# Attention, experts and a gated layer on one core: the experts' second product token-major with 512 columns moving, batches cut into 256 and 320 tokens, the last sums transposed by blocks

## The chip, the core and the metric

The kernel runs on one core of a Trainium2 chip. The metric is the device time of one execution in microseconds, as the median of several runs. The core has TensorE (PE in the rows; PEld is its weight load), VectorE (DVE), ScalarE (ACT), GpSimd (POOL) and SyncE (SP), each with its own instruction queue in program order; they wait for one another through semaphores. Matmul results go to PSUM, which has eight banks of 512 fp32 columns on 128 partitions.

## What is computed

Four batches of 576 tokens, eight heads of 64. Attention goes through 32 packed queries per head; then four experts with a hidden width of 1024, weighted by token; then a layer of width 2048 with s * relu^2 + b.

```python
def _attn_ref(q, k, v, p):
    p_packed = sm_attn(p, k, v)
    return sm_attn(q, p_packed, p_packed)

def _moe_ref(x, domain_probs, w1, w2):
    p = domain_probs / (domain_probs.sum(-1, keepdims=True) + 1e-09)
    out = np.zeros((N, D), dtype=np.float32)
    for e in range(E):
        h = np.maximum(x @ w1[e], 0.0)
        out += p[:, e:e + 1] * (h @ w2[e])
    return out

def _moe2_ref(x, w_in, w_out, s, b):
    r = np.maximum(x @ w_in, 0.0)
    return (s * (r * r) + b) @ w_out
```

N = 2304 tokens, D = 512, E = 4, F = 1024, d_ff = 2048; inputs fp32.

## The kernel before

Every large product is made of three fp32r matmuls: each operand is split into an upper part (a copy rounded to fp32r) and a lower part (the rest), and high x low, high x high and low x high are added up in PSUM.

The order of all work is written out by hand. The main loop runs over `ua`: expert e, batch bi, half hf of the batch's 576 tokens (288 each), hidden block f of 128, 256 steps in all. In step i it first issues what the table `weave` has for i (`run(i)`), then by `advance()` the first product `m1` of step i + 2, then the second product `m2` of step i. `m1` (line 708): six matmuls with a block of the folded first weight stationary and 288 token columns moving into a bank of two (`h`); ScalarE writes the relu's upper part (line 718), VectorE the lower (line 719). `m2` (line 736): for each of four 128-wide output blocks m three matmuls, a block of the second weight stationary, 288 token columns moving, into four banks `acc0` to `acc3`, which add up over the eight f of a half. The result lies with output features on partitions and tokens in columns.

At a half's last f the four banks are emptied: for expert 0 VectorE multiplies by the token's weight into `x2` (line 760), for later experts into `y` (line 751), and POOL adds `y` to `x2` (line 762). The weights per token lie along the columns, so they are broadcast over all partitions: `expert_weights` (woven into step 3) norms them with four small VectorE operations and writes them to DRAM; `load_pb` loads them, once for every expert and batch, broadcast.

Expert 0's steps are woven with the attention of the next batch: `at_s1` (scores of the packed queries, line 189), `at_exp1`, `at_a1t` (TensorE transposes, line 237), `at_pv`, `at_pt`, `at_s2` (line 306), then on VectorE and POOL `at_s2t` to `at_fin`, which writes the batch's `a2`, the moving operand of `m1`. The halves of `at_s2` to `at_fin` are those of `m1`. Experts 1 to 3 are woven with the folding of the next first weight (lines 502 and 548), the split of the second weight (lines 573, 576) and the preparation of the last layer's weights.

The last layer is `m3` (line 860: seven combinations of quarters of x, 384 columns moving) and `m4` (line 896: 128 tokens stationary, 512 columns of the output weight moving). `m3` starts ten units early (`EARLY`), inside the last ten steps of the main loop; `m4` of a pair of token tiles starts 18 units after its first `m3`. `x_sum` and `xs_parts` (line 804, 805) make `m3`'s operands from `x2`, six tiles of 384 tokens with features on partitions. `gate` queues four operations (ScalarE 814, VectorE 817, ScalarE 824, VectorE 828) in a list `later`, of which `go_on`, called in each `m3`, issues one per entry.

Of the kernel before, what the change touches and what calls it, by code (L numbers as in the profile page):

```python
# [8 lines left out]
F32 = mybir.dt.float32  # L9
# [10 lines left out]
def attention_experts_mlp_kernel(  # L20
# [78 lines left out]
    pn_dram = dram.tile([E, NT], F32, name="pn_dram")  # L99
# [216 lines left out]
    def at_s2t(bi, h, gs=(0, 1)):  # L316
        for g in gs:
            nc.vector.transpose(
                out=stt["sc", bi, h][:, blocks((g,))[0], :32],
                in_=stt.pop(("s2", bi, h, g))[:, :HT],  # L320
# [5 lines left out]

    def at_max2(bi, h, gs=(0, 1), eng=nc.gpsimd):
        j, n = blocks(gs)
        sc = stt["sc", bi, h][:, j, :32]
        m = att.tile([P, NJ, 1], F32, tag="mx", bufs=2, name=f"mx_{bi}{h}{gs[0]}")[:, j, :]  # L330
# [3 lines left out]
    def at_exp2(bi, h, gs=(0, 1)):  # L334
        sc = stt["sc", bi, h][:, blocks(gs)[0], :32]
        nc.scalar.activation(sc, sc, AF.Exp, scale=scale)

    def at_norm2(bi, h, gs=(0, 1), eng=nc.gpsimd):
        j, n = blocks(gs)
        sc = stt["sc", bi, h][:, j, :]  # L340
        r = att.tile([P, NJ, 1], F32, tag="r2", bufs=2, name=f"r2_{bi}{h}{gs[0]}")[:, j, :]
# [8 lines left out]
    def at_a2t(bi, h, gs=(0, 1)):  # L350
        j, n = blocks(gs)
        tag, bufs, size = ("a1", 2, S) if (bi, h) == (0, 0) else ("t", 3, NJ * 33)
# [335 lines left out]
    pb_t = {}  # L688

    def load_pb(e, bi):  # L690
        t = wa.tile([P, S], F32, tag="pb", bufs=2, name=f"pb_{e}{bi}")
        nc.sync.dma_start(
            out=t, in_=pn_dram[e, bi * S : (bi + 1) * S].partition_broadcast(P)
        )
        pb_t[e, bi] = t

    hh = {}

    def hid(dt, tag, bufs, name):
        return wa.tile([P, HT], dt, tag=tag, bufs=bufs, name=name)  # L700

    def m1(e, bi, hf, f):
        t = ps_h.tile([P, 512], F32, tag="h", name=f"h_{e}{bi}{hf}{f}")
        tok = slice(hf * HT, (hf + 1) * HT)
# [11 lines left out]
        xh = hid(F32R, "hh", 3, f"hh_{e}{bi}{hf}{f}")[:, :HT]  # L716
        xl = hid(F32R, "hl", 3, f"hl_{e}{bi}{hf}{f}")[:, :HT]
        nc.scalar.activation(xh, t[:, :HT], AF.Relu)  # L718
        nc.vector.scalar_tensor_tensor(  # L719
            out=xl, in0=t[:, :HT], scalar=0.0, in1=f32(xh), op0=ALU.max, op1=ALU.subtract  # L720
        )
        hh[e, bi, hf, f] = (xh, xl)

    acc = {}
    x2 = {}

    def m2(e, bi, hf, f):
        xh, xl = hh.pop((e, bi, hf, f))
        wh, wl = w2_t[e, f]
        if f == 0:  # L730
            for m in range(KB):
                acc[m] = ps_acc.tile([P, 512], F32, tag=f"acc{m}", name=f"acc_{e}{bi}{hf}{m}")
        for m in range(KB):
            col = slice(m * P, (m + 1) * P)
            for n, (w, x) in enumerate(((wl, xh), (wh, xh), (wh, xl))):
                nc.tensor.matmul(  # L736
                    acc[m][:, :HT],
                    lhsT=w[:, col],
                    rhs=x,
                    start=(f == 0 and n == 0),  # L740
# [561 lines left out]
```

## Time and profile before

| | us |
|---|---|
| median of 3 runs | 1096.07 (1095.29 to 1096.73) |
| the profiled execution | 1094.97 |
| its span, first to last instruction | 1093.2 |
| TensorE busy | 1080.1 |
| VectorE, ScalarE, POOL busy | 670.3, 399.5, 288.7 |

Expert 0's steps run from about 26 to 221 us, the others to 391, 553 and 720, the last layer after that. In a row of a group the mean is the length of one instruction; for overlapping matmuls the distance from start to start in the timeline is what one costs. What stands in brackets at the end of a timeline row is idle time of that engine just before it, and what ended it.

### The profile page before, as it was taken

The page shows a single profiled execution, that of the slowest core. Times are in us where ns is not written, and L with a number is a line of the kernel's source. Part 1 is how long each engine was busy: PE and PEld are TensorE (multiplying, and loading weights), DVE is VectorE, ACT ScalarE, POOL GpSimd, SP SyncE. Part 2 cuts the span into 40 slices and gives each one's busy share as a digit, 9 for nine tenths or more (in the row PEclk, how much of TensorE's full clock was granted, in tenths as well). Part 3 has the DMA queues.
Part 4 walks back from the last instruction along what each step waited for, and adds up shares of the span by engine and source line. Part 5 has one row for each costly group of instructions (what it writes and reads, how often), then busy time and mean ns, then how long its engine had stood idle before and what let it go on. Part 6 is the DMA issues. An engine that isn't in the chain of part 4 may idle for free.

```text
span 1093.2 us, 19304 instructions
## 1 busy us (share of the span) xinstructions
PE 1080.1 (99%) x7588; PEld 1004.6 (92%) x7588; DVE 670.3 (61%) x1235; ACT 399.5 (37%) x798; POOL 288.7 (26%) x344
## 2 busy tenths in 40 slices
PE   8999999999999999999999999999999999999998
PEld 5788889999999999999999999989899999999987
DVE  7875764567566446556456634489845766775555
ACT  3433223553443343433433313255632332342121
POOL 1530203134322244224244343264111120210000
PEclk9999999999999999999999999999999999999999
DMA  9742221133226684774685431346766555655532
GB/s 279 213 131 58 52 85 36 29 100 115 70 66 243 219 228 134 218 231 155 223 220 156 139 98 72 150 165 249 289 200 220 184 205 173 214 205 189 191 116 87
DMA packets 68971, 175.14 MB, mean 160 GB/s; under 512 B 11408, under 2 KB 28048, under 8 KB 68880
## 3 DMA queue, kind: packets, MB, share of 16 engines
q1 hardware_dynamic: 68032, 172.79, 49.3%
q8 instruction: 60, 0.98, 0.4%
q10 hardware_dynamic: 848, 1.11, 0.4%
q14 instruction: 31, 0.25, 0.1%
HBM read 127.44 MB, written 46.44 MB: 159 GB/s over the span
## 4 chain that ended last, share of the span: by engine, by line
PE 94%; DVE 3%; POOL 1%; ACT 1%; issue 1%; DVEq 0%; POOLq 0%; ACTq 0%
PE acc L736 36%; PE h L708 19%; PE o L896 18%; PE h L860 15%; PE pp L502 1%; PE s L189 1%; PE pp L548 1%; PE s L306 1%; PE pv L255 1%; PE pw L400 1%; ACT a L226 1%; PE warm L947 1%; PE tr L237 0%; POOL x L762 0%; DVE kT L150 0%
## 5 line engine op out<-in xcount | busy, mean ns | idle before, releaser
L736 PE MATMUL acc<-hl,w2h 128*128 128x288 f32 x1024 | 303.0, 296 | 0.0
L736 PE MATMUL acc<-hh,w2l 128*128 128x288 f32 x1024 | 302.5, 295 | 0.5 <-POOL w2l L576 0.5
L736 PE MATMUL acc<-hh,w2h 128*128 128x288 f32 x1024 | 302.6, 296 | 0.0
L708 PE MATMUL h<-a,w1p 128*128 128x288 f32 x1536 | 250.4, 298 | 1.1 <-DVE hl L719 0.9
L719 DVE SCALAR_TENSOR_TENSOR hl<-h,hh 128x288 fp32r<-128x288 f32 x256 | 116.3, 454 | 188.8 <-ACT hh L718 187.6
L708 PEld LDWEIGHTS h<-a,w1p 128*128 128x128 f32 x1536 | 216.6, 188 | 16.7 <-issue 11.4
L896 PE MATMUL o<-wo,gg 128*128 128x512 f32 x864 | 223.1, 392 | 1.9 <-DVE gg L828 1.9
L860 PE MATMUL h<-xs,wop 128*128 128x384 f32 x1008 | 203.3, 337 | 0.7 <-DVE y L751 0.7
L736 PEld LDWEIGHTS acc<-hh,w2l 128*128 128x128 f32 x1024 | 192.3, 188 | 0.9 <-POOL w2l L576 0.7
L736 PEld LDWEIGHTS acc<-hl,w2h 128*128 128x128 f32 x1024 | 192.9, 188 | 0.0
L860 PEld LDWEIGHTS h<-xs,wop 128*128 128x128 f32 x1008 | 180.1, 188 | 13.8 <-DVE y L751 1.4
L736 PEld LDWEIGHTS acc<-hh,w2h 128*128 128x128 f32 x1024 | 192.7, 188 | 0.0
L896 PEld LDWEIGHTS o<-wo,gg 128*128 128x128 f32 x864 | 160.2, 188 | 26.3 <-DVE gg L828 2.7
L718 ACT ACTIVATE hh<-h 128x288 fp32r<-128x288 f32 x256 | 104.5, 408 | 213.1 <-PE h L708 206.4
L762 POOL TENSOR_TENSOR x<-x,y 128x288 f32<-128x288 f32 (+2 forms) x144 | 88.6, 651 | 162.4 <-DVE y L751 162.1
L814 ACT ACTIVATE yy<-yy 128x768 f32<-128x768 f32 x48 | 40.2, 838 | 114.6 <-DVE yy L880 114.6
L880 DVE TENSOR_TENSOR yy<-h,uv 128x384 f32<-128x384 f32 x96 | 51.0, 552 | 47.9 <-PE h L860 47.8
L824 ACT ACTIVATE gg<-yy,b_sb 128x768 fp32r<-128x768 f32 x48 | 44.8, 934 | 37.5 <-DVE yy L817 36.2
L828 DVE SCALAR_TENSOR_TENSOR gg<-yy,b_sb,gg 128x768 fp32r<-128x768 f32 x48 | 55.2, 1150 | 1.2 <-ACT gg L824 1.2
L576 POOL TENSOR_TENSOR w2l<-w2r,w2h 128x512 fp32r<-128x512 f32 x32 | 41.8, 1306 | 52.4 <-ACT w2h L573 45.2
L817 DVE SCALAR_TENSOR_TENSOR yy<-yy,s_sb 128x768 f32<-128x768 f32 x48 | 51.2, 1067 | 0.0
L685 POOL TENSOR_TENSOR wo<-wo 128x512 fp32r<-128x512 f32 x16 | 24.0, 1507 | 102.2 <-ACT wo L684 102.2
(374 smaller groups left out, 978.0 us busy)
## 6 DMA issues: line engine op xcount, KB each, us to landing
xs<-xs_dram SPq DMA_DIRECT2D x63, 768.0 KB, 4.3
w1p_dram<-w1o SPq DMA_DIRECT2D x32, 512.0 KB, 3.7
w1p<-w1p_dram SPq DMA_DIRECT2D x128, 128.0 KB, 4.4
xs_dram<-xs SPq DMA_DIRECT2D x21, 768.0 KB, 3.4
w2r<-in_moe_w_dram SPq DMA_DIRECT2D x32, 256.0 KB, 4.8
w1r<-in_moe_w_dram SPq DMA_DIRECT2D x12, 512.0 KB, 5.1
q<-in_q_dram SPq DMA_DIRECT2D x16, 288.0 KB, 7.7
pb<-pn_dram SPq DMA_DIRECT2D x16, 288.0 KB, 4.5
```

Of the source, the lines that this page charges most:

```text
L576: nc.gpsimd.tensor_tensor(out=lo, in0=raw_t.pop((e, f)), in1=f32(hi), op=ALU.subtract)
L708: nc.tensor.matmul(t[:, :HT], lhsT=w1p_block(e, bi, f, gi, w), rhs=a2[bi][:, x, gi, tok], start=(n == 0), stop=(n == 3 * G - 1),)
L718: nc.scalar.activation(xh, t[:, :HT], AF.Relu)
L719: nc.vector.scalar_tensor_tensor(out=xl, in0=t[:, :HT], scalar=0.0, in1=f32(xh), op0=ALU.max, op1=ALU.subtract)
L736: nc.tensor.matmul(acc[m][:, :HT], lhsT=w[:, col], rhs=x, start=(f == 0 and n == 0), stop=(f == NF - 1 and n == 2),)
L762: nc.gpsimd.tensor_tensor(out=dst, in0=dst, in1=y[:, a - t0 : z - t0], op=ALU.add)
L817: nc.vector.scalar_tensor_tensor(out=y, in0=y, scalar=s_sb, in1=y, op0=ALU.mult, op1=ALU.mult)
L824: nc.scalar.activation(t[:, 0], y, AF.Identity, bias=b_sb)
L828: nc.vector.scalar_tensor_tensor(out=t[:, 1], in0=y, scalar=b_sb, in1=f32(t[:, 0]), op0=ALU.add, op1=ALU.subtract)
L860: nc.tensor.matmul(ps, lhsT=w[:, a, col], rhs=x[:, z, m, :], start=(n == 0), stop=(n == 3 * HK - 1),)
L880: nc.vector.tensor_tensor(out=dst, in0=ps, in1=src, op=ALU.add)
L896: nc.tensor.matmul(o_acc[i], lhsT=lhsT, rhs=w, start=(f == 0 and n == 0), stop=(f == FG - 1 and n == 2),)
```

## The change

- `m2` becomes token-major: 128 tokens of the hidden values are stationary, all 512 columns of the second weight's row block move. A bank holds one tile of 128 tokens by 512 features; the four banks are used in rotation.
- 576 is no multiple of 128, so a batch is cut at 256 (even batches: 256 and 320 tokens) or 320 (odd: 320 and 256), and the 64 tokens left at the end of an even batch share a tile with the first 64 of the next. `m1` of these steps writes its hidden values in two pieces; `rest` holds the shared tile's eight blocks. `m2` has six matmuls in a step, and nine in the first half of an odd batch.
- A token's weight now is a value per partition: `p_tok` is made by four TensorE transposes and one ScalarE copy at the end of `expert_weights`, whose VectorE operations work on 18 partitions. The trip through DRAM, `load_pb` and `y` are gone. `m2_out` empties a bank by one VectorE operation, which also adds the sum so far (`xt`).
- In the last expert the sum is written back to PSUM, transposed there by VectorE in 32x32 blocks into `xt`, and `x_turn` moves the blocks by ScalarE copies to their places in `x2`: 16 copies for each of six groups of three tiles, two in each step, queued in `later` and issued at the end of a step.
- `raw0` and `p_rows` take the place of smaller tiles; `x2_0` lies where the first batch's `a2` was.

The diff, cut to what the steps of the prediction speak of (the attention functions take their slices from `part`, `width` and `pieces` in the same way throughout):

```diff
+    def part(bi, h):
+        a = 256 + 64 * (bi % 2)
+        return slice(a * h, a + (S - a) * h)
...
     def at_s2(bi, h, tags="mm"):
...
                     nc.tensor.matmul(
-                        ps[g][half(c ^ bi % 2), :HT],
+                        ps[g][half(c ^ bi % 2), :n],
                         lhsT=stt["sbd", bi, c][half(g), e, :],
-                        rhs=kqT["q", bi, c][half(g), e, h * HT : (h + 1) * HT],
+                        rhs=kqT["q", bi, c][half(g), e, part(bi, h)],
...
     def m1(e, bi, hf, f):
...
-                    t[:, :HT],
+                    t[:, : width(bi, hf)],
                     lhsT=w1p_block(e, bi, f, gi, w),
-                    rhs=a2[bi][:, x, gi, tok],
+                    rhs=a2[bi][:, x, gi, part(bi, hf)],
...
+        todo = [(x, t[:, : 2 * P])]
+        if bi % 2 and not hf:
+            todo = [(x, t[:, 64 : 64 + 2 * P])]
+            todo.append(([y[:, 64:] for y in rest[f]], t[:, :64]))
+        elif hf and not bi % 2:
+            y = wa.tile([P, 2, P], F32R, tag="rest", bufs=NF, name=f"rest_{e}{bi}{f}")
+            rest[f] = y[:, 0], y[:, 1]
+            todo.append(([y[:, :64] for y in rest[f]], t[:, 2 * P : 2 * P + 64]))
+        for (hi, lo), src in todo:
+            nc.scalar.activation(hi, src, AF.Relu)
+            nc.vector.scalar_tensor_tensor(
+                out=lo, in0=src, scalar=0.0, in1=f32(hi), op0=ALU.max, op1=ALU.subtract
+            )
+
+    def m2(e, bi, hf, f):
+        wh, wl = w2_t[e, f]
+        own = hh.pop((e, bi, hf, f))
+        t0 = (bi * S + P // 2 * (bi % 2) + hf * 2 * P) // P
+        do = [(t0 + i, [y[:, i * P : (i + 1) * P] for y in own]) for i in range(2)]
+        if bi % 2 and not hf:
+            do.append((t0 - 1, rest.pop(f)))
+        for j, (xh, xl) in do:
+            if f == 0:
+                n = acc["n"] = (acc.get("n", -1) + 1) % KB
+                acc[j] = ps_acc.tile([P, DM], F32, tag=f"acc{n}", name=f"acc_{e}{j}")
+            for n, (x, w) in enumerate(((xh, wl), (xh, wh), (xl, wh))):
+                nc.tensor.matmul(
+                    acc[j], lhsT=x, rhs=w,
+                    start=(f == 0 and n == 0), stop=(f == NF - 1 and n == 2),
+                )
+            if f == NF - 1:
+                m2_out(e, j)
...
+    def m2_out(e, j):
+        t, p1 = acc.pop(j), p_tok[:, e, j : j + 1]
...
+        dst = x if e < E - 1 else t
         nc.vector.scalar_tensor_tensor(
+            out=dst, in0=t, scalar=p1, in1=x, op0=ALU.mult, op1=ALU.add
+        )
+        if e == E - 1:
+            nc.vector.transpose(out=x, in_=t)
+            done.append(j)
+            if all(NS * i + n in done for n in range(NS)):
+                later.append([(x_turn, i, a, h) for a in range(4) for h in range(2)])
+
+    def x_turn(i, a, h):
...
+        r = slice(32 * a, 32 * a + 32)
+        src = xt[i][r].rearrange("j t (m q c) -> j q m t c", m=KB, q=4)
+        dst = x2[i].rearrange("j m (t b c) -> j b m t c", t=NS, b=4)
+        for q in (2 * h, 2 * h + 1):
+            nc.scalar.activation(dst[32 * q : 32 * q + 32, a], src[:, q], AF.Copy)
...
         def expert_weights():
...
+            dp = p_rows[:NB, 0].rearrange("j (a e) -> j a e", e=E)
+            ds = p_rows[:NB, 2, :P]
+            nc.vector.reduce_sum(ds, dp, axis=AX.X)
+            nc.vector.tensor_scalar(ds, ds, 1e-9, None, ALU.add)
+            nc.vector.reciprocal(ds, ds)
+            pn = p_rows[:NB, 1].rearrange("j (e a) -> j e a", e=E)
             nc.vector.tensor_tensor(
+                out=pn.rearrange("j e a -> j a e"), in0=dp,
+                in1=ds.unsqueeze(2).to_broadcast([NB, P, E]), op=ALU.mult,
+            )
+            t = bank("p_tok")[:, : E * NB].rearrange("a (e j) -> a e j", e=E)
+            for e in range(E):
+                nc.tensor.transpose(t[:, e, :], pn[:, e, :], ident[:NB, :NB])
+            nc.scalar.activation(p_tok, t, AF.Copy)
...
-                at(s0 + 8, load_pb, ne, nb)
...
             m2(*u)
+            if later and i < pos(0):
+                go_on()
             if pos(0) <= i:
                 m3(*ub[i - pos(0)])
```

## Rows read from the trace of the kernel before

**Rows 1.** The page: busy time by engine, granted clock by slice, chain by line.
```profile
PE 1080.1 (99%) x7588; PEld 1004.6 (92%) x7588; DVE 670.3 (61%) x1235; ACT 399.5 (37%) x798; POOL 288.7 (26%) x344
...
PEclk9999999999999999999999999999999999999999
...
PE acc L736 36%; PE h L708 19%; PE o L896 18%; PE h L860 15%; PE pp L502 1%; PE s L189 1%; PE pp L548 1%; PE s L306 1%; PE pv L255 1%; PE pw L400 1%; ACT a L226 1%; PE warm L947 1%; PE tr L237 0%; POOL x L762 0%; DVE kT L150 0%
```

**Rows 2.** Groups by line and shape: instruction, count, busy us, mean ns, idle before.
```profile
L736 PE MATMUL acc<-hl,w2h 128*128 128x288 f32 x1024 | 303.0, 296 | 0.0
...
L896 PE MATMUL o<-wo,gg 128*128 128x512 f32 x864 | 223.1, 392 | 1.9 <-DVE gg L828 1.9
L860 PE MATMUL h<-xs,wop 128*128 128x384 f32 x1008 | 203.3, 337 | 0.7 <-DVE y L751 0.7
```

**Rows 3.** Timeline of PE, 500 to 512 us: start, length, instruction, count.
```profile
500.48 0.96 PE L708 MATMUL h<-a,w1p 128*128 128x288 f32 x6
...
502.87 0.96 PE L708 MATMUL h<-a,w1p 128*128 128x288 f32 x6
```

**Rows 4.** Timeline of PE in the last layer, 734 to 740 and 1074 to 1090.
```profile
734.88 1.20 PE L860 MATMUL h<-xs,wop 128*128 128x384 f32 x6
...
738.42 1.31 PE L896 MATMUL o<-wo,gg 128*128 128x512 f32 x5
...
1073.69 15.80 PE L896 MATMUL o<-wo,gg 128*128 128x512 f32 x69
```

**Rows 5.** Timeline of PE, 222 to 224 us: matmuls of 256 columns.
```profile
223.09 0.28 PE L548 MATMUL pp<-w1h,ptpl 128*128 128x256 f32 x1
...
223.80 0.42 PE L708 MATMUL h<-a,w1p 128*128 128x288 f32 x2
```

**Rows 6.** Timeline of DVE and of PE around step 3, 36 to 46 us.
```profile
36.66 2.28 DVE L150 STREAM_TRANSPOSE kT<-k 128x576 f32<-128x576 f32 x2
...
39.99 0.28 DVE L976 TENSOR_TENSOR pn<-dp,ds 128x72 f32<-128x72 f32 x1
...
38.99 1.19 PE L189 MATMUL s<-kT,pbd 64*64 64x288 f32 x12 [1.50 <-DVE kT L150]
40.11 1.06 PE L708 MATMUL h<-a,w1p 128*128 128x288 f32 x6
```

**Rows 7.** Groups by line and shape: prices of DVE and ACT operations.
```profile
L719 DVE SCALAR_TENSOR_TENSOR hl<-h,hh 128x288 fp32r<-128x288 f32 x256 | 116.3, 454 | 188.8 <-ACT hh L718 187.6
L718 ACT ACTIVATE hh<-h 128x288 fp32r<-128x288 f32 x256 | 104.5, 408 | 213.1 <-PE h L708 206.4 <-DVE sc L318 3.3 <-DVE y L751 2.0
...
L912 DVE TENSOR_TENSOR o_sb<-o,o_sb 128x512 f32<-128x512 f32 x53 | 36.2, 684 | 14.6 <-PE o L896 14.6
...
L573 ACT ACTIVATE w2h<-w2r 128x512 fp32r<-128x512 f32 x32 | 20.1, 632 | 21.1 <-PE acc L736 17.8 <-DMA w2r<-in_moe_w_dram 3.2
...
L355 DVE STREAM_TRANSPOSE at<-sc 128x576 f32<-128x576 f32 x6 | 4.7, 777 | 2.9 <-POOL sc L346 2.9
```

**Rows 8.** Timeline of PE, 34 to 51 us: transposes of the packed attention.
```profile
47.02 0.75 PE L237 MATMUL tr<-ident,a 128*128 128x128 f32 x4 [0.51 <-ACT a L226]
```

**Rows 9.** Timeline, 221 to 230 and 672 to 684 us: two waits of PE.
```profile
228.33 0.37 PE L736 MATMUL acc<-hh,w2l 128*128 128x288 f32 x1 [0.49 <-POOL w2l L576]
...
672.33 4.37 POOL L762 TENSOR_TENSOR x<-x,y 128x96 f32<-128x96 f32 x8 [3.43 <-DVE y L751]
...
680.61 1.06 PE L708 MATMUL h<-a,w1p 128*128 128x288 f32 x6 [0.90 <-DVE hl L719]
```

**Rows 10.** Hand-over: timeline 715 to 743; stretches (PE, PEld, DVE, ACT, POOL busy).
```profile
719.27 1.93 DVE L805 TENSOR_TENSOR xs<-x,xs 128x768 fp32r<-128x768 f32 x1
...
719.72 1.23 PE L860 MATMUL h<-xs,wop 128*128 128x384 f32 x6
...
734.06 0.98 PE L896 MATMUL o<-wo,gg 128*128 128x512 f32 x3 [1.88 <-DVE gg L828]
...
720.00:745.00 25.00, 22.39 (x115) 19.91 (x114) 23.80 (x26) 14.63 (x21) 16.30 (x11) 1.00 0.39 157
```

More of the change, by code (lines that the diff above doesn't have):

```diff
@@ L98, in attention_experts_mlp_kernel, with width @@
     own = att.tile([P, 2, D], F32, name="own")
-    pn_dram = dram.tile([E, NT], F32, name="pn_dram")
+    p_tok = const.tile([P, E, NT // P], F32, name="p_tok")
+    HB = 10
+    XB = NT3
+    def part(bi, h):
+        a = 256 + 64 * (bi % 2)
+        return slice(a * h, a + (S - a) * h)
+    def width(bi, h):
+        t = part(bi, h)
+        return t.stop - t.start
     kq_in, kqT, v_in, pbd = {}, {}, {}, {}
@@ L318, in at_s2t @@
             nc.vector.transpose(
-                out=stt["sc", bi, h][:, blocks((g,))[0], :32],
-                in_=stt.pop(("s2", bi, h, g))[:, :HT],
+                out=stt["sc", bi, h][:, pieces(bi, h, (g,))[0], :32],
+                in_=stt.pop(("s2", bi, h, g))[:, : width(bi, h)],
             )
@@ L325, in blocks, with pieces @@
         return slice(gs[0] * NJ // 2, gs[0] * NJ // 2 + n), n
+    def pieces(bi, h, gs):
+        n = width(bi, h) // 32
+        return slice(gs[0] * n, (gs[0] + len(gs)) * n), len(gs) * n
     def at_max2(bi, h, gs=(0, 1), eng=nc.gpsimd):
[L328 removed]
+        j, n = pieces(bi, h, gs)
         sc = stt["sc", bi, h][:, j, :32]
[L330 removed]
+        m = att.tile([P, 2 * HB, 1], F32, tag="mx", bufs=2, name=f"mx_{bi}{h}{gs[0]}")[:, j, :]
         nc.vector.reduce_max(m.rearrange("a j o -> a (j o)"), sc, axis=AX.X)
@@ L350, in at_a2t @@
     def at_a2t(bi, h, gs=(0, 1)):
-        j, n = blocks(gs)
-        tag, bufs, size = ("a1", 2, S) if (bi, h) == (0, 0) else ("t", 3, NJ * 33)
+        j, n = pieces(bi, h, gs)
+        tag, bufs, size = ("a1", 2, S) if (bi, h) == (0, 0) else ("t", 3, 2 * HB * 33)
         t = att.tile([P, size], F32, tag=tag, bufs=bufs, name=f"at_{bi}{h}{gs[0]}")[:, : n * 32]
@@ L685, in wo_parts @@
         nc.gpsimd.tensor_tensor(out=lo, in0=f32(lo), in1=f32(hi), op=ALU.subtract)
[L688 to L700, printed above, removed]
+    later = []
+    hh, rest, acc, xt, x2 = {}, {}, {}, {}, {}
     def m1(e, bi, hf, f):
         t = ps_h.tile([P, 512], F32, tag="h", name=f"h_{e}{bi}{hf}{f}")
-        tok = slice(hf * HT, (hf + 1) * HT)
         n = 0
@@ L719, in m1 @@
+    done = []
+    def m2_out(e, j):
+        t, p1 = acc.pop(j), p_tok[:, e, j : j + 1]
+        i = j // NS
+        if i not in xt:
+            xt[i] = keep.tile([P, NS, DM], F32, tag="x2", bufs=XB, name=f"xt_{i}")
+        x = xt[i][:, j % NS]
+        if e == 0:
+            nc.vector.tensor_scalar(x, t, p1, None, ALU.mult)
+            return
+        dst = x if e < E - 1 else t
         nc.vector.scalar_tensor_tensor(
-            out=xl, in0=t[:, :HT], scalar=0.0, in1=f32(xh), op0=ALU.max, op1=ALU.subtract
+            out=dst, in0=t, scalar=p1, in1=x, op0=ALU.mult, op1=ALU.add
@@ L721, in m1 @@
         )
[L722 to L740, printed above, removed]
-                    stop=(f == NF - 1 and n == 2),
-                )
-        if f < NF - 1:
-            return
-        t0 = bi * S + hf * HT
-        cuts = sorted({t0, t0 + HT} | {c for c in range(0, NT, T3) if t0 < c < t0 + HT})
-        for m in range(KB):
-            if e > 0:
-                y = hid(F32, "y", 3, f"y_{e}{bi}{hf}{m}")
-                pb = pb_t[e, bi][:, hf * HT : (hf + 1) * HT]
-                nc.vector.tensor_tensor(out=y[:, :HT], in0=acc[m][:, :HT], in1=pb, op=ALU.mult)
-            for a, z in zip(cuts, cuts[1:]):
-                i = a // T3
-                if i not in x2:
-                    x2[i] = keep.tile([P, KB, T3], F32, tag="x2", bufs=NT3, name=f"x2_{i}")
-                dst = x2[i][:, m, a - i * T3 : z - i * T3]
-                src = acc[m][:, a - t0 : z - t0]
-                if e == 0:
-                    pb = pb_t[e, bi][:, a - bi * S : z - bi * S]
-                    nc.vector.tensor_tensor(out=dst, in0=src, in1=pb, op=ALU.mult)
-                else:
-                    nc.gpsimd.tensor_tensor(out=dst, in0=dst, in1=y[:, a - t0 : z - t0], op=ALU.add)
```

56 lines of the change are left out of this document (29 added, 27 removed).

## Prediction

> **What bounds the kernel now.** I read the page from the top: the share of busy time, the granted clock, then the chain that ended last. The reader should see that TensorE is busy for 99% of the span, that its granted clock shows a 9 in all 40 slices (the upper of its two levels, 2.4 GHz), and that the chain lies on TensorE for nearly its whole length: 36% on the second product (line 736), 19% on the first (708) [rows 1]. So the time is the sum of TensorE's periods, and another engine counts only where TensorE waits for it. The row of a group gives 296 ns for a matmul [rows 2], but matmuls overlap, so this is no price. A price is the distance between starts. From one group of six first-product matmuls to the next, a whole step of 6 + 12 matmuls of 288 columns, it is 502.87 - 500.48 = 2.39 us, or 132.8 ns each [rows 3].
>
> **The second product.** Now each of 32 halves (4 experts, 4 batches, 2) has 8 steps of 12: 3072 matmuls of 288 columns, at 132.8 ns 408.0 us. Afterwards there are 4 experts x 8 hidden blocks x 18 token tiles x 3 = 1728 of 512, the same 884,736 columns. The last product (`m4`, line 896) has this very form, 128x128 stationary and 512 moving: 69 in a row take (15.80 - 0.39)/68 = 226.6 ns each, groups of five among other work (1.31 - 0.39)/4 = 230 ns [rows 4]. (0.39 us is the length of one matmul's own row [rows 2].) The new groups are of six or nine, so I take 228.5, between them: 394.8 us. Gain 13.2 us; the ends are 226.6 (16.4) and 230 (10.6).
>
> The Trainium skill, TensorE: Matmul & The Clock Gate, section Back-to-back issue gap, speaks against the change: it gives columns/2.4 + 2.5 ns, 122.5 ns for 288 and 215.8 for 512, so that leaving out 1344 matmuls saves 3.4 us and not 13.2. The trace disagrees at both sizes (132.8 and 226.6 to 230 [rows 3, 4]); what that rule would do to the time is the second rival below.
>
> **The first product.** 1536 matmuls of 288 become 768 of 256 and 768 of 320. Six of 256 columns take 223.80 - 223.09 = 0.71 us, 118 ns each [rows 5]; 384 columns take (1.20 - 0.34)/5 = 172 ns [rows 2, 4]. No row has 320: it lies between 132.8 and 172, on the line from 256 to 384 at 145, and I take 146.5, since that one group of 384 is a short one. 768 x (118 + 146.5) = 203.1 against 204.0: gain 0.9 (a loss of 4 to a gain of 6, if the 320 is off by 6 ns).
>
> **Uneven steps.** A step is now 6 x 118 + 6 x 228.5 = 2.08 us in most halves, 2.25 where 320 columns meet two tiles, and 2.94 where a tile is shared by two batches. What is woven between steps has 0.31 us less cover per short step. Attention of batches 1 and 3 is woven into short steps: TensorE waits at its transposes for ScalarE, 0.51 us [rows 8], and batches 2 and 3 do the same. +0.3 each for 1 and 3; for 2, whose chain lies in long steps, -0.2: +0.4 us.
>
> **The opening.** The expert weights of step 3 now end in four TensorE transposes and a ScalarE copy, ahead of the scores of batch 1 in TensorE's order. VectorE has a queue there: the transposes of k (36.66, 2.28 us) end at 38.94, the weights' own four operations follow and end at 40.27, and the scores that wait for k start at 38.99, the first product at 40.11 [rows 6]. Afterwards those four work on 18 partitions, but on 512, 128, 128 and 512 elements in a row: two at 0.684 [rows 7], two at some 0.33 (between the 0.28 of a small one [rows 6] and 0.684), 2.0 us. Starting at 39.0, behind k's, they end near 41.0; four transposes and the copy, whose bank the scores need, add 0.7 (four of 128 columns take 0.75 [rows 8]); all 16 score matmuls 1.3 (twelve take 1.1 [rows 6]). The first product starts near 43.0, 2.9 later. The savings of steps 0 to 2 (0.93 us) and some 0.1 of a shorter first part vanish in that wait as well: +3.9 us (ends 2 and 6). Behind the waiting transposes stand the scores, the fifth first product and all after them; ScalarE and VectorE get ahead meanwhile, so nothing further is late.
>
> **What goes.** 16 broadcast loads of weights leave SP's queue, and POOL loses its sums at line 762. Today TensorE is held up at 228.33 for 0.49 us, at a half's first product into an accumulator (the row names the split of the second weight, but VectorE is just emptying that bank), and at 680.61 for 0.90, since POOL's eight sums, 4.37 us from 672.33, put off the weight sums that ScalarE waits for ahead of its relu [rows 9]. The new accumulators rotate over four banks with two or three in use, so they are free a half earlier, and the sums are gone: -1.4 us. VectorE's emptying is 18 x 0.684 per expert instead of 32 of 288 columns at some 0.45 [rows 7], nothing on the path. The extra 64-token pieces (one small ScalarE and VectorE operation in half the steps) hide under 2.25 and 2.94 us of TensorE.
>
> **The last expert.** Each tile costs VectorE 0.684 for the sum and 0.70 for the transpose (0.777 for 576 [rows 7]). Then ScalarE turns it, 16 copies of 384 elements on 32 partitions per group of three tiles, two a step; by the operations on 288 (0.408) and 512 (0.632) [rows 7] 0.50 each. They stand in ScalarE's order ahead of the next step's relu (0.408), after which VectorE takes 0.454 [rows 7] before the bank of the first product is free. After three tiles into short steps: VectorE's 3 x 1.38 = 4.15 us begin some 1.1 before the half's end and are done 3.0 after it; two turns, one woven copy, relu and the lower part follow: 3.0 + 1.0 + 0.63 + 0.41 + 0.5 = 5.5, needed at 2 x 2.08 = 4.16: 1.4 us. Two tiles into short steps, without a woven copy: 0.3. Long steps cover it. Together +1.7 (0 to 5).
>
> **The hand-over.** The second product ends at T = 719.72. VectorE is then in a 1.93 us operation until T + 1.5 [rows 10]; two sums and two transposes take it to T + 4.25, and only then can ScalarE begin the last 16 turns, queued ahead of the gates. To the first gate's upper part there are ten turns (5.0) and eight other operations at that stretch's mean, 14.63/21 = 0.70 [rows 10]: T + 14.9; its lower part, at VectorE's mean of 0.92 there: T + 15.8. Today the last product gets it at 734.06, T + 14.3 [rows 10], after waiting 1.88. So +1.5 us there; of the six turns left, 3.0 us, which delay the copies of the next operands, I count 1.8: +3.3 (ends -1 and 6).
>
> **Sum.** -13.2 - 0.9 + 0.4 + 3.9 - 1.4 + 1.7 + 3.3 = -6.2. The profiled execution took 1094.97 (span 1093.2 and 1.8 around it), the runs' median is 1096.07, 1.1 above. So 1088.8 by the profile, 1089.9 as a median. My ends, combined as independent ones, give 1083 to 1098 for this case, chance 0.60.
>
> **Rivals.** (1) The waits of opening, last expert and hand-over are hidden, because queues run ahead elsewhere: -13.2 - 0.9 - 1.4 gives 1080.6. For it: TensorE waits today for only some 13 us of 1093 [rows 1]; against it: the order in the queues is fixed by the program. 0.22. (2) A column costs at 512 what it costs at 288 (132.8/288 = 0.461 ns, 236 ns a matmul): the main gain is nil, 1103. The 226.6 to 230 of [rows 4] speak against it. 0.09. By the 3.4 us of the Trainium skill it would be 1099.7. (3) Slower: ScalarE becomes the bound in the last expert. A short step holds two turns, a relu (0.41) and, in two steps of three, a woven operation of 512 (0.63, so 0.42 on average); it outlasts 2.08 us once a turn costs over 0.62. If copies that cross from one group of 32 partitions to another cost double (1.0), each of 16 short turning steps takes 2.83 instead of 2.08, 12 us, and the hand-over's sixteen another 8: 1110. No row has such a copy across partitions of this size. 0.09.
>
> **How the numbers follow.** The likeliest case gives 1089.9. The range takes in the first rival down to 1079 and the second at 1103; what is left out is the third and part of the first, under 0.2. A measurement of this kernel can tell about 0.2%, or 2.2 us, from no change. Of the forecast's 0.60 0.48 lies under 1093.9, 0.10 within 2.2 us, 0.02 above; rival 1 is faster, 2 and 3 slower: 0.70, 0.10, 0.20.
>
> **What would show it.** The second product's rows: 1728 of 512, 227 to 230 between starts, six in some 1.37 us. First products six in 0.71 or 0.88. A hole in TensorE before the transposes of the expert weights, until about 41, waiting for VectorE. No wait for an accumulator at a half's end. In the last expert, waits of first products for VectorE at starts of short halves. Between 720 and 745 ScalarE near 90% busy, with last products waiting for gates. If the second product's period is over 234, or turning copies cost over 0.6 us, I am wrong.

## The result and the profile after

The changed kernel takes 1111.54 us (median; 1110.32 to 1112.62) beside 1096.4 for the kernel before: 1.0139 times as long, interval 1.0122 to 1.0157. I had forecast 1089.9 and a range up to 1103: wrong in sign, and out of the range. The kernel that the experiments led to takes 1093.15, 0.9978 times the kernel before (0.9968 to 0.9988).

The page of the changed kernel, as [rows 1] and [rows 2] for before:

```profile
span 1108.5 us, 16823 instructions
...
PE 1078.5 (97%) x6248; PEld 918.5 (83%) x6248; DVE 694.3 (63%) x1309; ACT 467.7 (42%) x1023; POOL 198.4 (18%) x200
...
PE 83%; DVE 8%; ACT 5%; issue 2%; DMA 2%; SPq 1%; POOL 0%; ACTq 0%; DVEq 0%
PE acc L755 28%; PE o L929 18%; PE h L717 16%; PE h L893 15%; ACT x L795 1%; PE pp L518 1%; DVE hl L739 1%; PE s L318 1%; DVE xt L778 1%; DMA v<-in_v_dram 1%; ACT hh L738 1%; DVE acc L774 1%; PE pp L564 1%; PE s L200 1%; PE pv L266 1%
...
L755 PE MATMUL acc<-w2h,hh 128*128 128x512 f32 x512 | 201.9, 394 | 0.0
```

The chain by engine in the kernel before:

```profile
PE 94%; DVE 3%; POOL 1%; ACT 1%; issue 1%; DVEq 0%; POOLq 0%; ACTq 0%
```

The chain has left TensorE: 83% of it lies there instead of 94%, 8% is on VectorE and 5% on ScalarE. The second product (now line 755) went from 36% of the chain to 28%; that does not measure its price, which fell by about 10 us of 1100 (below), but shows how much of the chain now runs over other engines. TensorE's own records lost 1.6 us of busy time, and the span grew by 15.3. The new time is waiting, and turns (`ACT x L795`), sums (`acc L774`) and transposes (`xt L778`) stand on the path.

Where it went, by distances between the first second products of the experts. In the kernel before these lie at 30.31, 228.33, 396.31 and 558.20 us. The first row starts at TensorE's first matmul; "hand-over" runs from the end of the second product to the third product's 181st matmul, and the last row from there to the start of the last matmul. The columns to the right are experiments told below (us).

| stretch | before | after | e1 | e3 | e4 | e5 | f1 | f2 | h3 | h4 |
|---|---|---|---|---|---|---|---|---|---|---|
| up to the first | 28.86 | 28.44 | 28.80 | 29.46 | 29.13 | 28.51 | 29.39 | 28.76 | 32.15 | 29.06 |
| expert 0 | 198.02 | 203.62 | 200.52 | 203.22 | 200.29 | 202.84 | 203.14 | 196.67 | 197.86 | 197.08 |
| expert 1 | 167.98 | 168.18 | 168.21 | 168.20 | 168.25 | 168.05 | 168.21 | 168.09 | 168.10 | 168.09 |
| expert 2 | 161.89 | 159.41 | 159.41 | 159.41 | 159.41 | 159.41 | 159.41 | 159.41 | 159.41 | 159.41 |
| expert 3 | 161.51 | 165.19 | 165.04 | 160.67 | 161.68 | 161.41 | 160.86 | 159.72 | 159.52 | 161.70 |
| hand-over | 39.89 | 46.74 | 46.62 | 40.83 | 40.80 | 46.72 | 40.81 | 40.79 | 40.80 | 46.76 |
| last layer | 329.49 | 331.21 | 331.21 | 331.21 | 331.21 | 331.21 | 331.21 | 331.21 | 331.21 | 331.21 |

Expert 2, where TensorE has no wait in either kernel, is 2.5 us shorter: the gain exists. Expert 0 loses 5.6, expert 3 3.7, the hand-over 6.9, the last layer 1.7, and expert 1 gains nothing.

**The steps themselves** came out as worked out. Timeline of TensorE, the last expert (start, length, instruction; the second products between are left out):

```profile
572.98 1.04 PE L717 MATMUL h<-a,w1p 128*128 128x320 f32 x6
575.24 1.04 PE L717 MATMUL h<-a,w1p 128*128 128x320 f32 x6
...
606.88 1.04 PE L717 MATMUL h<-a,w1p 128*128 128x320 f32 x6
609.82 1.04 PE L717 MATMUL h<-a,w1p 128*128 128x320 f32 x6
...
628.82 0.88 PE L717 MATMUL h<-a,w1p 128*128 128x256 f32 x6
630.93 0.88 PE L717 MATMUL h<-a,w1p 128*128 128x256 f32 x6
```

Steps of 2.26, 2.94 and 2.11 us, where I had 2.25, 2.94 and 2.08.

**The opening.** Timeline of VectorE and of TensorE, 36 to 48 us:

```profile
36.29 2.28 DVE L161 STREAM_TRANSPOSE kT<-k 128x576 f32<-128x576 f32 x2
...
38.75 0.65 DVE L1004 TENSOR_REDUCE p_rows<-p_rows 18x128 f32<-18x512 f32 x1
39.43 1.03 DVE L1005 TENSOR_SCALAR p_rows<-p_rows 18x128 f32<-18x128 f32 x1
40.49 0.94 DVE L1006 RECIPROCAL p_rows<-p_rows 18x128 f32<-18x128 f32 x1
41.47 1.02 DVE L1008 TENSOR_TENSOR p_rows<-p_rows 18x512 f32<-18x512 f32 x1
```

```profile
42.63 0.58 PE L1014 MATMUL p_tok<-ident,p_rows 18*128 18x18 f32 x4 [7.00 <-DVE p_rows L1008]
43.15 2.58 PE L200 MATMUL s<-kT,pbd 64*64 64x288 f32 x16
45.66 1.31 PE L717 MATMUL h<-a,w1p 128*128 128x256 f32 x6
```

TensorE idles 7.00 us for the expert weights, and the next 16 score matmuls take 2.58 where twelve took 1.19 [rows 6]: the granted clock fell to 0.5 (1.2 GHz) at 39.59, in that hole, and came back at 46.41. The first product starts at 45.66, 5.55 later than before.

**The last expert.** ScalarE and VectorE, 622 to 628, and the wait that follows on TensorE:

```profile
624.62 1.06 ACT L795 ACTIVATE x<-xt 32x384 f32<-32x384 f32 x2 [4.76 <-DVE xt L778]
625.71 0.38 ACT L738 ACTIVATE hh<-h 128x256 fp32r<-128x256 f32 x1
```

```profile
626.12 0.42 DVE L739 SCALAR_TENSOR_TENSOR hl<-h,hh 128x256 fp32r<-128x256 f32 x1 [1.02 <-ACT hh L738]
```

```profile
626.60 0.98 PE L717 MATMUL h<-a,w1p 128*128 128x256 f32 x6 [0.95 <-DVE hl L739]
```

ScalarE is idle for 4.76 us ahead of two turns, because these wait for VectorE's transpose; the relu behind them (line 738) could have run from 622.16, when the six matmuls that it reads end (start 621.29, 0.87 us), and comes at 625.71. The lower part, the bank, and TensorE follow. One second product waits too, for a bank out of which VectorE transposes, at a half's start:

```profile
600.21 0.47 PE L755 MATMUL acc<-w2l,rest 128*128 128x512 f32 x1 [0.80 <-DVE xt L778]
```

**The hand-over.** The waits of TensorE from 716 to 752 us, then the busy time by stretch (columns as in [rows 10]):

```profile
731.68 9.12 PE L893 MATMUL h<-xs,wop 128*128 128x384 f32 x42 [3.15 <-DVE xt L778]
740.97 0.62 PE L893 MATMUL h<-xs,wop 128*128 128x384 f32 x2 [0.17 <-ACT xs L837]
742.42 0.98 PE L893 MATMUL h<-xs,wop 128*128 128x384 f32 x4 [0.83 <-DVE xs L838]
746.08 1.61 PE L929 MATMUL o<-wo,gg 128*128 128x512 f32 x3 [2.22 <-DVE gg L861]
```

```profile
725.00:745.00 20.00, 14.71 (x69) 13.05 (x67) 14.46 (x17) 14.75 (x25) 11.77 (x7) 0.91 0.32 128
```

TensorE waits 3.15 us for the transpose of the very last tile: the third product takes over the bank in which that tile lies. After it come waits for operands that stand behind turns on ScalarE, and for the lower part of the first gate, which gets to TensorE at 746.08, 19.8 after the end of the second product instead of 14.3 [rows 10]. The clock is at 0.5 twice here, from 732.49 and from 746.15, 3.41 us each.

### The profile page after: what moved, and what is told of

It is laid out like the page before. It is cut to its first block, busy times and chain, and to the rows that moved or that the text cites. A ratio compares the mean times of both kernels' runs of the same rounds, so it can differ in the third digit from the quotient of the medians.

```text
span 1108.5 us, 16823 instructions
## 1 busy us (share of the span) xinstructions
PE 1078.5 (97%) x6248; PEld 918.5 (83%) x6248; DVE 694.3 (63%) x1309; ACT 467.7 (42%) x1023; POOL 198.4 (18%) x200
## 4 chain that ended last, share of the span: by engine, by line
PE 83%; DVE 8%; ACT 5%; issue 2%; DMA 2%; SPq 1%; POOL 0%; ACTq 0%; DVEq 0%
PE acc L755 28%; PE o L929 18%; PE h L717 16%; PE h L893 15%; ACT x L795 1%; PE pp L518 1%; DVE hl L739 1%; PE s L318 1%; DVE xt L778 1%; DMA v<-in_v_dram 1%; ACT hh L738 1%; DVE acc L774 1%; PE pp L564 1%; PE s L200 1%; PE pv L266 1%
## 5 line engine op out<-in xcount | busy, mean ns | idle before, releaser
L717 PE MATMUL h<-a,w1p 128*128 128x320 f32 (+1 forms) x1536 | 252.2, 299 | 7.5 <-DVE hl L739 4.5
L755 PE MATMUL acc<-w2h,hh 128*128 128x512 f32 x512 | 201.9, 394 | 0.0
L755 PE MATMUL acc<-w2l,hh 128*128 128x512 f32 x512 | 201.7, 394 | 0.0
L755 PE MATMUL acc<-w2h,hl 128*128 128x512 f32 x512 | 200.2, 391 | 0.0
L739 DVE SCALAR_TENSOR_TENSOR hl<-h,hh 128x256 fp32r<-128x256 f32 x256 | 107.6, 420 | 142.3 <-ACT hh L738 141.7
L738 ACT ACTIVATE hh<-h 128x256 fp32r<-128x256 f32 x256 | 97.0, 380 | 109.6 <-PE h L717 107.4
L755 PEld LDWEIGHTS acc<-w2h,hl 128*128 128x128 f32 x512 | 96.2, 188 | 22.1
L755 PEld LDWEIGHTS acc<-w2l,hh 128*128 128x128 f32 x512 | 96.4, 188 | 11.9
L755 PEld LDWEIGHTS acc<-w2h,hh 128*128 128x128 f32 x512 | 96.4, 188 | 10.8
L795 ACT ACTIVATE x<-xt 32x384 f32<-32x384 f32 x96 | 50.2, 523 | 20.5 <-DVE xt L778 18.9
```

Of the source, the lines that this page charges most:

```text
L717: nc.tensor.matmul(t[:, : width(bi, hf)], lhsT=w1p_block(e, bi, f, gi, w), rhs=a2[bi][:, x, gi, part(bi, hf)], start=(n == 0), stop=(n == ...
L738: nc.scalar.activation(hi, src, AF.Relu)
L739: nc.vector.scalar_tensor_tensor(out=lo, in0=src, scalar=0.0, in1=f32(hi), op0=ALU.max, op1=ALU.subtract)
L755: nc.tensor.matmul(acc[j], lhsT=x, rhs=w, start=(f == 0 and n == 0), stop=(f == NF - 1 and n == 2),)
L795: nc.scalar.activation(dst[32 * q : 32 * q + 32, a], src[:, q], AF.Copy)
```

## The experiments

Theory W: the prices are right, and the loss is a few waits that come from the fixed order in the queues, with the clock falling behind some of them. Its rival P: the new form is dearer than its rows, so that time taken out of one wait turns up in another.

**e1: the transposes of the tokens' weights at step 6.**

```diff
+        def token_weights():
+            pn = p_rows[:NB, 1].rearrange("j (e a) -> j e a", e=E)
             t = bank("p_tok")[:, : E * NB].rearrange("a (e j) -> a e j", e=E)
             for e in range(E):
...
                 at(3, expert_weights)
+                at(6, token_weights)
```

> One part is moved: the four transposes that turn the tokens' weights (p_tok) and ScalarE's copy of them go from step 3 to step 6 of the opening; their DVE work stays where it is. Theory W (the prices of the products came out as forecast, and the loss is waits in the fixed order of the queues): the wait of 7.00 us ahead of the transposes goes, the clock no longer falls to 0.5 at 39.59, and the first two products that had waited start about 5 us earlier; 1111.5 falls by 5 to 8 us, to 1104 to 1106.5. Theory P (the new form of the products costs more than the rows say, and the waits only show where slack is taken up): PE finds the same time lost a few steps later, and the gain is under 2 us, above 1109.

1108.4 us, 1.0109 (1.0093 to 1.0126): 3.0 of span, between what W and P had forecast. The wait of 7.00 is gone, but another stood behind it, for keys that VectorE transposes. TensorE in this kernel:

```profile
39.00 1.44 PE L200 MATMUL s<-kT,pbd 64*64 64x288 f32 x12 [2.36 <-DVE kT L161]
40.36 1.65 PE L717 MATMUL h<-a,w1p 128*128 128x256 f32 x6
```

The clock still falls, for 3.41 us instead of 6.83. Counted from the first second product, the 19th starts 5.4 us earlier than in the changed kernel, the 37th only 3.1: the rest is lost again by then (54 us).

**e2: the accumulators' buffers taken in the order 0, 3, 2, 1**, so that the last tiles lie in banks which the third product takes later.

```diff
-                acc[j] = ps_acc.tile([P, DM], F32, tag=f"acc{n}", name=f"acc_{e}{j}")
+                acc[j] = ps_acc.tile([P, DM], F32, tag=f"acc{(0, 3, 2, 1)[n]}", name=f"acc_{e}{j}")
```

> Only the names of the four accumulators' buffers are rotated (0, 3, 2, 1), so that the last two tiles of the last expert lie in banks that the third product takes two tiles later. Theory W: the wait of 3.15 us at 731.68, for the emptying of the very last tile, goes; what is behind it (waits of 0.33 and 0.83 for the operands of the third product, 2.22 for a gate) may take up to half of it back: 1108 to 1110, 1.5 to 3.5 us below the changed kernel. Theory P: the stretch is limited by ScalarE's and VectorE's own work, and the wait moves on unchanged: within 1 us of 1111.5.

1111.31, 1.0138 (1.0123 to 1.0153): nothing. The wait of 3.15 has shrunk to 0.12, and the waits behind it grew from 3.2 to 5.0 us in all; TensorE in this kernel, 718 to 756 us:

```profile
736.93 0.62 PE L893 MATMUL h<-xs,wop 128*128 128x384 f32 x2 [1.20 <-ACT xs L837]
738.37 2.87 PE L893 MATMUL h<-xs,wop 128*128 128x384 f32 x10 [0.81 <-DVE xs L838]
742.61 1.01 PE L893 MATMUL h<-xs,wop 128*128 128x384 f32 x2 [1.38 <-ACT xs L837]
```

The clock also fell to 0.5, from 739.22 for 13.65 us. Two pairs below tell the same without that difference: with the turns on GpSimd and the clock at 1.0 the hand-over takes 40.80 us with the new order of banks (e4) and 40.83 without (e3); with the turns on ScalarE and two falls of 3.41 us it takes 46.76 with it (h4) and 46.72 without (e5). So the longest wait of the stretch was not its cause; another queue was equally late, and e3 and h4 show whose.

**e3: the turns on GpSimd.**

```diff
-            nc.scalar.activation(dst[32 * q : 32 * q + 32, a], src[:, q], AF.Copy)
+            nc.gpsimd.tensor_copy(dst[32 * q : 32 * q + 32, a], src[:, q])
```

> Only the turns of the last expert (the copies that put the transposed blocks into place) go from ScalarE to GpSimd. Theory W: ScalarE is then free for the relus, the waits at the starts of the last expert's halves (0.3 to 1.1 us, eight of them) shrink by about half, and the operands of the third product come earlier: 3 to 6 us below 1111.5, if GpSimd's copy of 32 x 512 takes under some 1.5 us (not shown in a trace so far); if it takes twice that, the last turns come late at the hand-over and it is slower by 3 to 8 us. Theory P: within 1 us of 1111.5.

1100.88, 1.0044 (1.0029 to 1.0059): 10.1 us of span, where I expected 3 to 6: 4.5 in the last expert and 5.9 in the hand-over. Groups of the changed kernel and of this one (count, busy, mean ns of one):

```profile
L795 ACT ACTIVATE x<-xt 32x384 f32<-32x384 f32 x96 | 50.2, 523 | 20.5 <-DVE xt L778 18.9
```

```profile
L795 POOL COPY x<-xt 32x384 f32<-32x384 f32 x96 | 62.6, 652 | 31.9 <-DVE xt L778 27.9
```

GpSimd is slower at a turn, 652 ns against 523, and yet 10 us are won: what cost the time was not a turn's length but what stood behind it. On GpSimd no relu stands behind, and TensorE's waits at this kernel's hand-over (1.52, 0.49 and 1.59 us) all name VectorE. The clock no longer falls at the hand-over. Such a fall alone does not make the hand-over long: in f3, h1 and h3 (below) it falls there for 3.41 us as well, and the stretch takes the same 40.80 as in e4 without a fall; in h2, with a fall of 6.83, it takes 42.34.

**e4: the three together.**

> The three edits together: the tokens' weights turned at step 6, the accumulators' buffers rotated, the turns on GpSimd. Theory W: the gains add up, 10 to 16 us below the changed kernel, 1096 to 1102. Theory P: at most 4 us below it, above 1107.

1098.57, 1.0019 (1.0010 to 1.0028). The gains of e1 and e3 add up (3.0 and 10.1 of span alone, 12.4 here); the banks again bring nothing that lasts. P is refuted: 12.4 us of span came back with not one matmul changed. But the kernel before is still not reached.

**f1: the weights' VectorE operations later too** (step 5, their transposes at step 7), on top of e4.

```diff
-                at(3, expert_weights)
-                at(6, token_weights)
+                at(5, expert_weights)
+                at(7, token_weights)
```

> To the three edits of the last kernel (1098.6) one is added: the four VectorE operations that make the tokens' weights move as well, from step 3 to step 5, with their transposes at step 7. Theory D (these 3.7 us on VectorE hold up the transposes of the next keys, for which TensorE waited 2.36 at 39.32 where the kernel before waited 1.50, and the clock falls behind that wait): the wait shrinks to about 1.5 and the clock stays at 1.0: 1.5 to 3 us less, 1095.6 to 1097. Rival (the next late thing is ScalarE's and VectorE's work on the first batch's scores, which did not move): within 0.7 us of 1098.6.

1100.24, 1.0050 (1.0033 to 1.0067): worse than e4, and both theories miss. The wait of 2.36 for the keys stays as it was, so those operations were not its cause, and a new wait appears. TensorE, then ScalarE, in this kernel:

```profile
56.84 1.13 PE L248 MATMUL tr<-ident,a 128*128 128x128 f32 x4 [2.31 <-ACT p_tok L1017]
```

```profile
56.44 0.22 ACT L738 ACTIVATE rest<-h 128x64 fp32r<-128x64 f32 x1 [4.15 <-DVE hl L739]
56.56 0.22 ACT L1017 ACTIVATE p_tok<-p_tok 128x72 f32<-128x72 f32 x1
```

The copy of the weights, 0.22 us, waits 4.15 behind the relu of 64 odd tokens (`rest`), which waits for VectorE to finish the lower part of the main tokens (`hl`): relu, lower part, relu, lower part, one after the other between two engines. VectorE comes to that lower part at 56.00, behind other work, two transposes of q of 1.24 and 1.26 us among it. The clock falls in this hole, at 55.33 for 6.83 us. These pieces were the extra operations that I had costed at nothing.

**f2: both relus first, then both lower parts**, on top of f1.

```diff
         for (hi, lo), src in todo:
             nc.scalar.activation(hi, src, AF.Relu)
+        for (hi, lo), src in todo:
             nc.vector.scalar_tensor_tensor(
```

> The last kernel with the emptying of the first product in another order: both relus of a step, then both lower parts, instead of part by part. Theory R (the 64 odd tokens' pieces form a chain of four hand-overs between ScalarE and VectorE, and TensorE waits for its end): the waits of 1.08, 0.33 and 0.96 in the short steps of the last expert shrink by 0.2 to 0.3 each, and here and there in the other experts: 0.5 to 1.5 us below the last kernel. Rival (VectorE's other work sets the end of the chain): within 0.3 us of it.

1093.15, 0.9978 (0.9968 to 0.9988): 7.1 us below f1, far more than expected. By the profiles 6.5 us are won in expert 0: two waits went, 2.31 and 1.07 us (the second for GpSimd's lower part of the second batch's tokens, at 83 us), and with them f1's fall of the clock, which may be most of the other 3.1 (not tested apart). There is no fall in the profiled execution before 1088.83 us of 1090.02. The last expert has hardly a wait left: at 159.72 it is 1.8 us shorter than before. Stretch 26 to 60 us of the changed kernel and of this one:

```profile
26.00:60.00 34.00, 26.32 (x221) 20.01 (x221) 25.73 (x53) 14.02 (x41) 16.88 (x21) 0.90 0.61 176
```

```profile
26.00:60.00 34.00, 30.54 (x283) 22.99 (x281) 29.92 (x62) 15.33 (x46) 17.03 (x21) 1.00 0.64 181
```

**e5: this order alone, in the changed kernel** (the same diff, without the others).

> The changed kernel (turns on ScalarE) with the new order of the relus alone. Theory R (the turns cost so much because they stand between the pieces of this chain): 2 to 5 us below 1111.5, a good part of what moving the turns to GpSimd gave. Rival (the turns cost their own 50 us of ScalarE's time wherever the pieces stand): less than 1 us.

1106.22, 1.0097 (1.0083 to 1.0112): 4.7 us of span, 3.8 in the last expert, none in the hand-over. Theory R holds, but only for the steps. These 3.8 us are largely the same time as the 4.5 that e3 wins there: with both edits, in f2, the last expert is 5.5 us shorter than in the changed kernel, not 8.3.

**h4: f2 with the turns back on ScalarE** (the diff of e3 undone).

> The kernel with five edits that took 1093.2, with one of them undone: the turns are back on ScalarE. Theory Q (the turns cost because ScalarE works them off ahead of the relus and of the operands of the third product, in the order of its queue, and mostly at the hand-over, whatever the order of the relus): 6 to 9 us more, 1099 to 1102, of it 5 to 6 at the hand-over and 1 to 3 in the last expert. Rival (once the relus come first the turns are hidden): within 2 us of 1093.

1103.58, 1.0062 (1.0050 to 1.0074): 9.0 of span more than f2, 2.0 in the last expert and 6.0 in the hand-over (the median lies 10.4 above f2's, beyond the forecast 6 to 9). TensorE at the hand-over in e5, then here, with the new order of banks:

```profile
727.07 9.12 PE L894 MATMUL h<-xs,wop 128*128 128x384 f32 x42 [3.16 <-DVE xt L779]
```

```profile
725.81 0.62 PE L894 MATMUL h<-xs,wop 128*128 128x384 f32 x2 [1.18 <-ACT xs L838]
727.25 3.28 PE L894 MATMUL h<-xs,wop 128*128 128x384 f32 x10 [0.82 <-DVE xs L839]
731.49 0.62 PE L894 MATMUL h<-xs,wop 128*128 128x384 f32 x2 [0.95 <-ACT xs L838]
732.92 0.98 PE L894 MATMUL h<-xs,wop 128*128 128x384 f32 x4 [0.82 <-DVE xs L839]
...
736.59 0.96 PE L930 MATMUL o<-wo,gg 128*128 128x512 f32 x3 [2.23 <-DVE gg L862]
```

The wait of 3.16 for the bank is 0.12 here, and the other waits of the stretch are 6.0 us instead of 3.2. Theory Q holds: the hand-over's loss is the place of the turns in ScalarE's queue, also with the four other edits in.

**h3: f2 with the weights' operations back at step 3** (transposes at step 6; the diff of f1 undone).

> The kernel that took 1093.2 with the four VectorE operations for the tokens' weights back at step 3 (their transposes at step 6). Theory: the wait of 2.36 us for the keys at 39 was the same with these operations at step 5, so that they are not its cause; the clock falls again behind this wait or it does not, and this alone decides: 1093 without a fall, 1094.5 to 1097 with one of 3.4 us or more. Rival (the place of the chain was worth the 5.5 us by which the order of the relus changed that kernel): 1097 to 1099.

1093.96, 0.9977 (0.9968 to 0.9985), level with f2: their place is indifferent once the relus come first. (The profiled execution of h3 lost 3.4 us ahead of the first second product, 1.24 of them waiting for a load of v.) Against e4, h3 differs by the order of the relus alone, and both show a fall of 3.41 us in the opening: the medians are 4.6 us apart, and the profiles show 2.4 in expert 0 and 2.2 in the last expert. That is the price of the order with the turns on GpSimd.

**f3, h1, h2: the border of the first two experts.** f3 moves the pair folds one step earlier (`s0 + 8` for `s0 + 9`) and splits GpSimd's lower part for the second batch's first tokens in two, on top of f2. h1 moves only the second pair's folds, without that split; h2 adds to h1 that the last two accumulators of expert 0 are emptied a step later. The diff shows h2 against f2, and h1 is its first pair of lines:

```diff
-                            at(s0 + 9 + 2 * c + x, fold_pair, ne, nb // 2, c, x)
+                            at(s0 + 9 - nb // 2 + 2 * c + x, fold_pair, ne, nb // 2, c, x)
...
+        if e == 0 and j >= NT // P - 2:
+            later.append([(min, 0, 0), (nc.vector.tensor_scalar, x, t, p1, None, ALU.mult)])
+            return
```

> The last kernel, with the pair folds for the second expert one step earlier, so that the last one stands ahead of the two accumulators' emptying, and with GpSimd's lower part for the second batch's first tokens split in two by its halves. If the two waits at the border of the experts (0.51 and 1.69 us) and the one at 80 (1.07) are what they look like, waits behind one VectorE queue and one GpSimd operation, 1.5 to 2.5 us go: 1093 to 1095, just below the kernel before. If the folds only move the wait to their new neighbours: within 0.5 us of the last kernel.

> The kernel that took 1093.2 with the pair folds one step earlier for the second pair alone (in the run before, both were moved: 5.1 us were lost in the first expert, where the folds then stand among ScalarE's splits of new weights, and 2.25 won in the second). If these are separate waits, 2 to 2.5 us less: 1090.5 to 1091.5. If the gain in the second expert hung on the first fold's place: within 0.5 us of 1093.2.

> The kernel before this one, and the emptying of the first expert's last two accumulators one step later, behind the fold's lower part on VectorE. If the wait of 1.7 us at the border of the first two experts is for VectorE's order alone, 1.2 to 2 us less again: 1089 to 1090. If it only changes places with another wait: within 0.5 us.

f3: 1095.12, 0.9998 (0.9989 to 1.0007), worse than f2: expert 0 is 5.2 us longer and expert 1 2.25 shorter. h1: 1093.2, 0.9975 (0.9965 to 0.9986). h2: 1094.19, 0.9977 (0.9968 to 0.9985). None beats f2. Waits of TensorE at the border in f2, then in h2:

```profile
228.92 0.98 PE L717 MATMUL h<-a,w1p 128*128 128x256 f32 x6 [0.49 <-DVE hl L740]
232.97 0.98 PE L717 MATMUL h<-a,w1p 128*128 128x256 f32 x6 [1.68 <-DVE hl L740]
```

```profile
231.74 0.98 PE L717 MATMUL h<-a,w1p 128*128 128x256 f32 x6 [0.48 <-DVE hl L740]
234.63 0.98 PE L717 MATMUL h<-a,w1p 128*128 128x256 f32 x6 [0.52 <-DVE hl L740]
237.76 0.98 PE L717 MATMUL h<-a,w1p 128*128 128x256 f32 x6 [0.77 <-DVE hl L740]
```

(h1 has 0.51 and 1.69 there, as f2.) One wait of 1.68 became two of 1.29 together: the order of VectorE's queue is worth 0.4 us, and the next operation in it is late instead. Of f3 I had read its 2.25 us in expert 1 as a gain; h1 has only 0.16 of it, so the second pair's folds alone do not bring it. In f3 two matmuls of the fold wait 1.10 us each for VectorE, at 210.72 and 224.89, and TensorE comes to the border 5 us later; the waits there are then 0.52 and 0.51. Whether they are shorter because VectorE has got ahead meanwhile was not tried. The wait at 80 us that f3's split was meant for is no longer there in f2.

## Why the prediction was wrong

**By stages.** With expert 2's 2.5 us as the gain of each expert, expert 0 lost 8.1 us to waits and the lower clock (I had 4.3 for opening and uneven steps), expert 1 2.7 (none), the last expert 6.2 (1.7), the hand-over 6.9 (3.3) and the last layer 1.7 (none).

**The second product: right in kind, 2.9 us too hopeful.** Between neighbours, 512 columns average 231.0 ns in the changed kernel and 288 averaged 133.3 in the one before: 1728 x 231.0 = 399.2 against 3072 x 133.3 = 409.5, a gain of 10.3 instead of 13.2, just past my lower end. The Trainium skill (TensorE: Matmul & The Clock Gate, section Back-to-back issue gap) gives the formula of the 3.4 us as the gap of an isolated matmul, which the prediction left unsaid; for a stream of weight loads and matmuls it has about 131 ns at 512 columns. The trace agrees with neither: it has 133.3 and 231.0 ns, and expert 2 alone is 2.5 us shorter. The first product brought nothing: by f2's means, 768 x (124.1 + 150.6) = 211.0 us, against 1536 x 136.9 = 210.3. That loss of 0.7 lies within the bounds that I gave for the gain of 0.9. The last layer, whose code is the same, lost 1.7 us: its 512s average 231.1 ns instead of 229.7, in groups of five 231.8 instead of 230.2, while the 98 in a row at the end take 227.1 in both kernels. No run told why, nor whether the second product's 231.0 has the same cause. (Steps of 2.08 us I put in "most halves"; they are 16 of 32, which changes no term.)

**The opening: mechanism right, size wrong.** The hole came where I put it, for the cause I named. I let it end "until about 41"; it ended at 42.63. Of that, 1.3 is two VectorE operations on 18 partitions x 128, which I put at 0.33 each "between the 0.28 of a small one and 0.684": they take 1.03 and 0.94, more than the reduction of four times the elements beside them (0.65). I had interpolated by size between two other operations. The first product came at 45.66 where I had 43.0, and 1.3 of that is the score matmuls at the lower clock; no step of mine asked what a hole of several microseconds does to the clock, though the kernel before had none to judge by.

**"The extra 64-token pieces hide": the step that failed.** I counted their length (one small operation on each engine) against 2.25 and 2.94 us of TensorE, and not their order. Each piece adds a round trip, since ScalarE's second relu stands behind VectorE's first lower part in the program and waits for it. e5 prices this at 4.7 us of span in the changed kernel, h3 against e4 at 4.6 with the turns on GpSimd; the 8.4 of span between f1 and f2 hold a fall of the clock besides.

**The last expert and the hand-over: the second step that failed.** The turn itself was well estimated (0.50; 0.523 measured), and I saw that it stands ahead of the relu. But I worked out one chain per half (1.4 and 0.3 us) and let everything else be hidden. Measured, the last expert lost 3.7 us where the product's gain alone (10.3 / 4) would have shortened it by 2.6, so its waits cost about 6 instead of 1.7. For the hand-over I had the lower part of the first gate ready at 15.8 us after the second product's end, with +1.5 for TensorE; it came at 19.8. I left out that the third product needs the bank of the last tile (3.15 us), and that its own operands (`xs`) wait behind turns. e5 and h4 show that mending the first alone moves the wait to the second; e3 and h4 show that the turns' place is worth 6 us here.

**What goes** went: no first product waits for POOL's sums any more, and no accumulator for its emptying at 228.33. A fold's lower part behind two emptyings, 0.48 + 1.68 at the border, took its place, and in the last expert an accumulator is waited for after all (0.80 at 600.21), which I had named as something that would not be seen.

**The rivals.** The third ended nearest, at 1110. But its condition was not met: a turn takes 0.523, not over 0.62, and ScalarE is busy for only 96.69 of 167 us in the last expert. What binds is not ScalarE's load but the order in which it serves; the slower engine (652 ns a turn) is 10 us better. So I got the engine and the place of that rival, and tied it to the wrong quantity. The first rival, all waits hidden at 1080.6, was out of reach at the measured prices: 1096.07 - 10.3 - 1.4 gives 1084.4, and the kernel without those waits stands at 1093.15. Between the two are 0.7 of the first product, 1.7 in the last layer, 2.2 at the border of the experts, 0.9 at the hand-over and, in expert 0, the wait for keys, 2.36 against 1.50 [rows 6]; the rest I did not trace. The two signs by which I would have called myself wrong, a period over 234 ns and a turn over 0.6 us, did not come (231.0 and 0.523): they watched the prices, and the order in the queues failed.

## What to carry to other kernels

An operation that is added to a busy queue is priced by what stands behind it and by what it waits for itself, not by its length: write the queue out in order, and ask of every engine that changes hands twice in a step whether it can do both halves of its work first. When a long wait is mended and nothing comes of it, look at which queue serves the next wait too; here the longest wait of the hand-over (3.15 us) was worth nothing, and a slower engine with nothing urgent behind it was worth ten. Cost small operations by the nearest row of the same shape and operation, not by elements.

## What had not been expected of the hardware

The granted clock fell from 1.0 to 0.5 (2.4 to 1.2 GHz) in holes of TensorE or shortly behind them, and came back 3.41 to 13.65 us later; in the kernel before it stays at 1.0 from 5.58 us to the end of the span. At the 7.00 us hole it fell for 6.83 us, at holes of 6.57 and 7.43 in the same place, in e2 and e5, for 10.24. But the same wait of 2.36 us at 39 us (at 42 in h3) goes with a fall in e1, e4, h1, h2 and h3, and with none in f1, f2, f3 and h4, and this does not go with the edits (f2 and h1 have the same opening). From f2 to h1 such a fall costs 1.4 us up to the 55th second product (32.17 against 33.62 us from the first). What decides stays open. Differences of that size are why I take the 1093.15, 1093.96, 1093.2 and 1094.19 us of f2, h3, h1 and h2, whose intervals overlap, as one result.

On 18 partitions, VectorE takes 1.03 and 0.94 us for 128 elements in a row (an addition of a scalar, 0.72 in e4, and a reciprocal), and 0.65 for a reduction from 512 to 128. The last of the four operations, 512 elements, takes 1.02 in the changed kernel and 2.13 in f1, where it stands two steps later. What doubles it was not tried.
